# A fused attention and mixer kernel on one core: the denominator's 1e-6 moves into the PSUM evacuation, reciprocals and division move one period ahead, and weight conversion runs in four places

## The chip, the core and the metric

The kernel runs on one core of one Trainium2 chip. The metric is the device time of one execution in microseconds (us). A core has a TensorE (PE, matmuls), a VectorE (DVE), a ScalarE (ACT), a GpSimd (POOL) and a SyncE (SP), which here only issues DMAs. Each engine works through its own instruction stream in order and waits on semaphores for the others, so an instruction that waits holds back all that stand behind it on its engine.

## The reference

Shapes: attention 8 batches x 8 heads, 576 tokens, head width 64, 128 features; then two mixer blocks on (8, 576, 512).

```python
def phi(x):
    proj = np.einsum('bhsd,df->bhsf', x, w_phi)
    proj = proj - np.max(np.abs(proj), axis=-1, keepdims=True)
    return np.concatenate([np.exp(proj), np.exp(-proj)], axis=-1)
q_p, k_p = (phi(q), phi(k))
kv = np.einsum('bhsf,bhsd->bhfd', k_p, v)
z = np.sum(k_p, axis=2)
num = np.einsum('bhsf,bhfd->bhsd', q_p, kv)
den = np.einsum('bhsf,bhf->bhs', q_p, z)[..., None] + 1e-06
x = num / den
# block 1: relu(x @ w_in) split in u, v; v normalised; u * (w_spatial @ v + b_spatial); @ w_out
# block 2: u = x + (x^T @ U @ V)^T; u + relu(u @ w_ch1) @ w_ch2
```

## The kernel before

All matmul operands are float32; where one is split into a high and a low part, a product is three matmuls (high*high, high*low, low*high). The program has three stages: attention over 32 pairs of heads (two heads of 64 side by side on 128 partitions), the first mixer block with the low-rank part of the second, and the channel matmuls. The change touches the first stage only, and the helper that converts the mixer's weights from 8-byte to 4-byte floats, which runs in small steps between the attention's instructions.

`attention` (L544) is software pipelined. Loop index `p` is a period: in period `p` the core projects keys and queries of pair `p+1` (`pk`, `pq`, L396 to L400, both into one PSUM tile), subtracts the largest magnitude of each row on DVE (`m`, `s`, L405 and L408), takes exponentials on ACT (`kp` L419; `qp` high part L438; `e` L447, whose difference from the high part is the low part, made by POOL at L450), transposes queries (`pt`, L428), sums keys times values of pairs `p` and `p+1` (`pkv`, L462 and L469), and multiplies queries of pairs `p-2` and `p-1` with those sums (`pn`, L497). Each pair has four such outputs g = 0 to 3, each of six matmuls of 288 columns into the same PSUM bank `pn`; the function `outputs` returns the evacuation of that bank into the tile `nd`, which the loop calls as `taken()`: ACT copies g = 0 and 2 (L506), DVE copies g = 1 and 3 (L505). The next output cannot start until the bank has been evacuated. `split_key_values` (L482 on ACT, then L483 on DVE) empties the single bank `pkv` into the two parts of `kv`, and only then can the sums of the next pair begin at L462.

Row 64 of `nd` holds the denominators. `undivided` sends them by DMA to a tile `den9` of 128 x 9 and the numerators to `x`; `reciprocals` adds 1e-6 (L526), takes reciprocals (L527), and sends them by a DRAM tile `rd` back as the broadcast tile `rec`; `finish` multiplies on POOL (L541) and stores `x` to DRAM tile `xd`. In period `p` these belong to pairs `p-2`, `p-3` and `p-4`.

The weight jobs stand in a list: 16 pieces of `w_in`, 4 blocks of `w_spatial`, its tail and the bias, 8 pieces of `w_out`. One job occupies one period (the tail and bias two). A converted piece is done in steps, called by `step(work)` at fixed places: `words` (ACT, L55), `rounded` (DVE L60, L64, L68, and at once the ACT square L70), `kept` (DVE L77, then the split into a high part on ACT and a low part on POOL, L129 and L132). A `w_spatial` block has one step at the end of the period: DVE cast L131, POOL low part L132; its DMA (L189) needs the staging tile that the POOL low part of the block before has to give back. `load_x` (L685 to L692) brings the first batch's divided tiles back during periods 8 to 13, with a POOL subtraction at L689.

`pin` keeps the attention's own instructions in program order on each engine; a scheduler places the weight work behind the pinned instruction it was called after, and orders the DMA issues on SP.

Of the kernel before, what the change touches and what calls it, by code (L numbers as in the profile page):

```python
# [9 lines left out]
F32 = mybir.dt.float32  # L10
# [3 lines left out]
AF = mybir.ActivationFunctionType  # L14
# [4 lines left out]
P = 128  # L19
# [8 lines left out]
def fetch_weight(nc, pool, dst, src, name, at=0, raws=None):  # L28
# [7 lines left out]
    p, n = shape[0], shape[1:]  # L36
# [21 lines left out]
    def rounded(low):  # L58
        bits = tile_view(I32, 1, "bits")
        nc.vector.tensor_scalar(  # L60
            out=bits, in0=hi, scalar1=3, scalar2=0x3FFFFFF8,
            op0=ALU.logical_shift_left, op1=ALU.bitwise_and,
        )
        nc.vector.scalar_tensor_tensor(  # L64
            out=bits, in0=hi, scalar=-0x40000000, in1=bits,
            op0=ALU.bitwise_and, op1=ALU.bitwise_or,
        )
        nc.vector.tensor_tensor(out=bits, in0=bits, in1=low, op=ALU.add)  # L68
        size = low.bitcast(F32)
        nc.scalar.activation(size, hi.bitcast(F32), AF.Square)  # L70
        return lambda: kept(bits.bitcast(F32), size)
# [19 lines left out]
class Mixer:  # L91
# [259 lines left out]
    def alloc_attention(self, es):  # L351
        tc, nc = self.tc, self.nc
        D, F = self.D, self.F
        self.pp = es.enter_context(tc.tile_pool(name="pp", bufs=1, space=PSUM))
        self.af = es.enter_context(tc.tile_pool(name="af", bufs=1))
        ap = self.ap = es.enter_context(tc.tile_pool(name="ap", bufs=1))

        self.wst = ap.tile([P, F], F32, name="wst")
        nc.scalar.dma_start(self.wst, self.w_phi)
        self.st = {}  # L360

    def load(self, p, w, bufs):
# [123 lines left out]
    def outputs(self, p, g, side, n, tag="pn"):  # L486


        nc, D, HS = self.nc, self.D, self.HS
        st = self.st[p]  # L490
        qp, kv = st["qp"], st["kv"]
        if g == 0:
            st["nd"] = self.af.tile([D + 1, 4, HS], F32, tag="nd", name=f"nd{p}", bufs=2)
        pn = self.pp.tile([P, 512], F32, tag=tag, name=f"pn{p}_{g}", bufs=1)[: D + 1, :HS]
        terms = [(0, 0, 0), (1, 0, 0), (0, 0, 1), (1, 0, 1), (0, 1, 0), (0, 1, 1)]
        for m, (k, q, i) in enumerate(terms):
            self.pin(nc.tensor.matmul(  # L497
                pn, kv[k][:, i, g // 2, :], qp[q][:, i, g * HS : (g + 1) * HS],
                start=(m == 0), stop=(m == len(terms) - 1),
            ))  # L500
            if m < n:
                next(side, None)
        nd = st["nd"][:, g, :]
        if g % 2:
            return lambda: self.pin(nc.vector.tensor_copy(nd, pn))  # L505
        return lambda: self.pin(nc.scalar.copy(nd, pn))  # L506

    def undivided(self, p):

# [12 lines left out]
    def reciprocals(self, p):  # L522

        nc, D, S = self.nc, self.D, self.S
        den9 = self.st[p].pop()
        self.pin(nc.vector.tensor_scalar_add(den9, den9, 1e-6))  # L526
        self.pin(nc.vector.reciprocal(den9, den9))  # L527
        rd = self.rd[p % 4]
        nc.sync.dma_start(rd, den9)
# [14 lines left out]
    def attention(self, jobs):  # L544
# [16 lines left out]
                    return f()  # L561
            return f

        for p in range(-1, n + 5):
            tag = "pn" if p < n else "kv"
            new, this, old, older = (0 <= i < n for i in (p + 1, p, p - 1, p - 2))
            if p + 2 < n:
# [13 lines left out]
                self.load(p + 2, "v", 2)  # L581
            if new:
                self.key_features(p + 1, 0)
            if 0 <= p - 4 < n:
                self.finish(p - 4)
            work = step(work)
            taken()
            if older:
# [5 lines left out]
                self.load(p + 2, "q", 1)  # L594
            if this:
                self.high_part(p, 0)
                self.low_part(p, 0)
            less()
            side = self.key_values(p + 1, 0) if new else iter(())
            taken = self.outputs(p - 1, 0, side, 3) if old else none  # L600
# [11 lines left out]
                self.low_part(p, 1)  # L612
            work = step(work, True)
            taken()
            if 0 <= p - 3 < n:
                self.reciprocals(p - 3)
            rest = [step(f) for f in rest]
            rest = [f for f in rest if f]
            if jobs and not work:
# [474 lines left out]
```

## Time and profile before

| what | value |
|---|---|
| median of 3 runs | 1727.13 us (1726.35 to 1729.3) |
| the profiled execution's own time | 1724.92 us |
| span of its trace | 1723.1 us |
| PE busy | 1657.6 us, 96% of the span |
| DVE, ACT, POOL busy | 774.5, 594.3, 469.7 us (45%, 34%, 27%) |
| mean granted TensorE clock | 0.988 |
| chain that ended last | PE 70%, DMA 6%, DVE 4%, ACT 2%, POOL 1% |

Shares over the whole span hide that the stages differ: DVE and POOL work mostly in the first quarter. In the profile, idle time of PE is time in which no matmul was in flight; a busy PE at a granted clock below 1 is slower than it could be.

### The profile page before, as it was taken

What the parts mean: (1) busy time and instruction counts of PE and PEld (TensorE: products, weight loads), DVE (VectorE), ACT (ScalarE), POOL (GpSimd) and SP (SyncE); (2) the same over time, 40 slices, a digit from 0 to 9 for tenths busy, and PEclk for the clock granted to TensorE, in tenths of its full rate; (3) what the DMA queues carried; (4) which work ended last, traced back from release to release, by engine and by line L of the source; (5) the groups of instructions that cost most, each with busy time, mean ns of one, the idle gap of its engine ahead of it and who ended that gap; (6) DMA issues with size and microseconds to landing.
All of it is one profiled execution on the core that took longest, in us unless ns stands there. A gap on an engine that the chain in (4) does not pass through costs nothing.

```text
span 1723.1 us, 26579 instructions
## 1 busy us (share of the span) xinstructions
PE 1657.6 (96%) x10824; PEld 1568.3 (91%) x10824; DVE 774.5 (45%) x1296; ACT 594.3 (34%) x1060; POOL 469.7 (27%) x402
## 2 busy tenths in 40 slices
PE   7989988998899999999999999999999999999999
PEld 7878877887797897888898999999999999999999
DVE  5888855884667566566637211121021121121121
ACT  4767755764434443443434111021120120110110
POOL 2567665675342342342330100000000000000000
PEclk9999998999999999999999999999999999999999
DMA  4576655663223332332225201001011011011000
GB/s 131 157 186 194 194 162 152 174 176 91 77 85 108 120 103 90 119 111 70 83 68 178 64 10 37 13 26 37 1 38 37 1 37 37 1 37 37 1 19 19
DMA packets 86142, 141.41 MB, mean 82 GB/s; under 512 B 18626, under 2 KB 41314, under 8 KB 86020
## 3 DMA queue, kind: packets, MB, share of 16 engines
q1 hardware_dynamic: 85876, 139.65, 27.5%
q8 instruction: 85, 1.39, 0.3%
q14 instruction: 37, 0.30, 0.1%
q10 hardware_dynamic: 144, 0.07, 0.0%
HBM read 93.25 MB, written 36.85 MB: 75 GB/s over the span
## 4 chain that ended last, share of the span: by engine, by line
PE 70%; DMA 6%; DVE 4%; ACT 2%; POOL 1%; issue 1%; SPq 0%; DVEq 0%; POOLq 0%; ACTq 0%
PE pc L653 23%; PE ph L653 23%; PE pv L653 5%; DMA raw_c<-in_w_ch 4%; PE px L653 4%; PE pu L653 4%; PE pn L497 2%; PE pkv L469 2%; PE pt L858 1%; PE py L862 1%; PE pz L653 1%; POOL xs L689 1%; PE pv L664 1%; PE px L664 1%; PE pt L428 1%
## 5 line engine op out<-in xcount | busy, mean ns | idle before, releaser
L653 PE MATMUL pc<-h,w 128*128 128x384 f32 x2304 | 403.8, 335 | 0.0
L653 PEld LDWEIGHTS pc<-h,w 128*128 128x128 f32 x2304 | 402.0, 188 | 0.0
L653 PE MATMUL ph<-us,w 128*128 128x384 f32 x2244 | 391.0, 334 | 0.0
L653 PEld LDWEIGHTS ph<-us,w 128*128 128x128 f32 x2244 | 389.2, 188 | 0.0
L906 ACT ACTIVATE h<-ph 128x384 fp32r<-128x384 f32 x187 | 92.0, 492 | 629.5 <-PE ph L653 626.6
L497 PE MATMUL pn<-qp,kv 128*65 128x288 f32 x768 | 211.9, 335 | 24.8 <-DVE nd L505 16.7
L132 POOL TENSOR_TENSOR us<-u,us 128x384 fp32r<-128x384 f32 x48 | 48.7, 1041 | 683.0 <-ACT us L129 674.1
L907 DVE SCALAR_TENSOR_TENSOR h<-ph,h 128x384 fp32r<-128x384 f32 x187 | 104.2, 557 | 273.1 <-ACT h L906 273.0
L450 POOL TENSOR_TENSOR qp<-e,qp 128x576 fp32r<-128x576 f32 x128 | 182.3, 1453 | 46.3 <-ACT e L447 46.3
L942 DVE TENSOR_TENSOR u<-pc,u 128x384 f32<-128x384 f32 x48 | 25.7, 558 | 363.6 <-PE pc L653 363.6
L469 PEld LDWEIGHTS pkv<-v,kp 128*128 128x128 f32 x1024 | 160.2, 201 | 0.0
L469 PE MATMUL pkv<-v,kp 128*128 128x65 f32 x1024 | 160.2, 261 | 0.0
L497 PEld LDWEIGHTS pn<-qp,kv 128*65 128x65 f32 x768 | 100.8, 142 | 30.2 <-DVE nd L505 23.4
L653 PE MATMUL pz<-wt,vn 128*128 128x288 f32 x768 | 112.4, 295 | 3.2 <-DVE u L799 3.2
L653 PEld LDWEIGHTS pz<-wt,vn 128*128 128x128 f32 x768 | 105.2, 188 | 3.7 <-DVE u L799 3.6
L653 PEld LDWEIGHTS pu<-xs,wi 128*128 128x128 f32 x768 | 102.8, 188 | 3.4 <-DVE v L716 2.7
L653 PE MATMUL pu<-xs,wi 128*128 128x288 f32 x768 | 103.4, 295 | 2.5 <-DVE v L716 2.5
L653 PE MATMUL px<-wo,g 128*128 128x512 f32 x384 | 94.1, 403 | 10.5 <-ACT g L129 10.5
L653 PEld LDWEIGHTS px<-wo,g 128*128 128x128 f32 x384 | 72.9, 194 | 29.2 <-ACT g L129 13.1
L653 PE MATMUL pv<-wi,xs 128*128 128x512 f32 x384 | 92.3, 394 | 0.0
L419 ACT ACTIVATE kp<-sk 128x1152 f32<-128x1152 f32 x64 | 74.2, 1161 | 36.1 <-DVE sk L408 33.5
L653 PEld LDWEIGHTS pv<-wi,xs 128*128 128x128 f32 x384 | 71.9, 188 | 15.8
(140 smaller groups left out, 1962.0 us busy)
## 6 DMA issues: line engine op xcount, KB each, us to landing
raw_c<-in_w_ch SPq DMA_DIRECT2D x32, 512.0 KB, 4.1
v<-in_v SPq DMA_DIRECT2D x32, 325.0 KB, 3.8
k<-in_kT SPq DMA_DIRECT2D x32, 320.0 KB, 3.7
q<-in_qT SPq DMA_DIRECT2D x32, 320.0 KB, 3.4
x<-nd SPq DMA_DIRECT2D x64, 144.0 KB, 2.5
rec<-rd SPq DMA_DIRECT2D x64, 144.0 KB, 3.2
xd<-x SPq DMA_DIRECT2D x32, 288.0 KB, 2.1
x<-xd SPq DMA_DIRECT2D x32, 288.0 KB, 3.0
```

Of the source, the lines that this page charges most:

```text
L132: return (nc.gpsimd if elo == "pool" else nc.vector).tensor_tensor(out=lo, in0=src, in1=hi, op=ALU.subtract)
L419: self.pin(self.nc.scalar.activation(kp, self.st[p]["sk"], AF.Exp, scale=1.0 - 2.0 * i))
L428: self.pin(nc.tensor.transpose(pt[:, at, :], s[:, u, :], self.ident))
L450: self.pin(nc.gpsimd.tensor_tensor(out=lo[:, c], in0=e[:, c], in1=hi[:, c], op=ALU.subtract))
L469: self.pin(nc.tensor.matmul(pkv[:, i, j, :], kp[:, j * NF + t, :], vb[:, u * D1 : (u + 1) * D1], start=False, stop=(j == 1 and t == NF - 1),))
L497: self.pin(nc.tensor.matmul(pn, kv[k][:, i, g // 2, :], qp[q][:, i, g * HS : (g + 1) * HS], start=(m == 0), stop=(m == len(terms) - 1),))
L653: self.nc.tensor.matmul(out, x, y, start=(start and i == 0), stop=(stop and i == len(terms) - 1))
L664: nc.tensor.matmul(out, x, y, start=(i == 0), stop=(i == len(terms) - 1))
L689: self.nc.gpsimd.tensor_tensor(out=lo, in0=x32, in1=hi, op=ALU.subtract)
L906: nc.scalar.activation(h[:, 0, :], ph, AF.Relu)
L907: nc.vector.scalar_tensor_tensor(out=h[:, 1, :], in0=ph, scalar=0.0, in1=h[:, 0, :], op0=ALU.max, op1=ALU.subtract,)
L942: nc.vector.tensor_tensor(out=u[:, f, :], in0=pcs[f], in1=u[:, f, :], op=ALU.add)
```

## The change

The diff below is complete. The 1e-6 is added while the output leaves PSUM, from a small tile `eps` that is 1e-6 on partition 64 and zero elsewhere; of the four outputs only g = 1 leaves through DVE, the other three through ACT as an Identity activation with a bias. The separate addition on `den9` is gone. `reciprocals` handles pair `p-2` and `finish` pair `p-3`, the loop is two periods shorter, and `finish` is called after `low_part(p, 0)` in place of before the step behind `key_features`. The square becomes a step of its own (`sized`), and a fourth call of `step` stands between the high part and the low part.

```diff
@@ fetch_weight
         nc.vector.tensor_tensor(out=bits, in0=bits, in1=low, op=ALU.add)
+        return lambda: sized(bits, low)
+
+    def sized(bits, low):
         size = low.bitcast(F32)
         nc.scalar.activation(size, hi.bitcast(F32), AF.Square)
         return lambda: kept(bits.bitcast(F32), size)
@@ alloc_attention
+        self.eps = ap.tile([P, 1], F32, name="eps")
+        nc.vector.memset(self.eps, 0.0)
+        nc.vector.memset(self.eps[D : D + 1, :], 1e-6)
@@ outputs
-        if g % 2:
-            return lambda: self.pin(nc.vector.tensor_copy(nd, pn))
-        return lambda: self.pin(nc.scalar.copy(nd, pn))
+
+        if g == 1:
+            return lambda: self.pin(nc.vector.tensor_scalar_add(nd, pn, self.eps[: D + 1, :]))
+        return lambda: self.pin(
+            nc.scalar.activation(nd, pn, AF.Identity, bias=self.eps[: D + 1, :])
+        )
@@ reciprocals
-        self.pin(nc.vector.tensor_scalar_add(den9, den9, 1e-6))
         self.pin(nc.vector.reciprocal(den9, den9))
@@ attention
-        for p in range(-1, n + 5):
+        for p in range(-1, n + 3):
@@
             if new:
                 self.key_features(p + 1, 0)
-            if 0 <= p - 4 < n:
-                self.finish(p - 4)
             work = step(work)
             taken()
@@
             if this:
                 self.high_part(p, 0)
+                work = step(work)
                 self.low_part(p, 0)
+            if 0 <= p - 3 < n:
+                self.finish(p - 3)
             less()
@@
             taken()
-            if 0 <= p - 3 < n:
-                self.reciprocals(p - 3)
+            if older:
+                self.reciprocals(p - 2)
```

PE's stream keeps the same instructions in the same order. On DVE, period 14 (`kv_14` is its pair) stood so before:

```order
L408 TENSOR_TENSOR sk_2136<-pk_2112,mk_2135 128x1152
L60 TENSOR_SCALAR bits_wi_0_2168<-raw_wi_0_2108 128x256
L64 SCALAR_TENSOR_TENSOR bits_wi_0_2168<-raw_wi_0_2108,bits_wi_0_2168 128x256
L68 ISA bits_wi_0_2168<-bits_wi_0_2168,low_wi_0_2140 128x512
L505 COPY nd_2063<-pn_3_2152 65x288
L483 TENSOR_TENSOR kv_14_2180<-pkv_2066,kv_14_2179 128x260
L405 TENSOR_REDUCE mq_2202<-pq_2183 128x9
L408 TENSOR_TENSOR sq_2203<-pq_2183,mq_2202 128x1152
L77 SCALAR_TENSOR_TENSOR w_wi_0_2107<-low_wi_0_2140,bits_wi_0_2168 128x256
L505 COPY nd_2206<-pn_1_2222 65x288
L526 TENSOR_SCALAR den_11_2031<-den_11_2031 128x9
L527 RECIPROCAL den_11_2031<-den_11_2031 128x9
```

and stands so now (`pn_3` is output g = 3; the number behind `den` is the pair):

```order
L414 TENSOR_TENSOR sk_2135<-pk_2111,mk_2134 128x1152
L60 TENSOR_SCALAR bits_wi_0_2165<-raw_wi_0_2107 128x256
L64 SCALAR_TENSOR_TENSOR bits_wi_0_2165<-raw_wi_0_2107,bits_wi_0_2165 128x256
L68 ISA bits_wi_0_2165<-bits_wi_0_2165,low_wi_0_2139 128x512
L489 TENSOR_TENSOR kv_14_2176<-pkv_2066,kv_14_2175 128x260
L411 TENSOR_REDUCE mq_2201<-pq_2179 128x9
L414 TENSOR_TENSOR sq_2202<-pq_2179,mq_2201 128x1152
L80 SCALAR_TENSOR_TENSOR w_wi_0_2106<-low_wi_0_2139,bits_wi_0_2165 128x256
L512 TENSOR_SCALAR nd_2205<-pn_1_2221,eps 65x288
L535 RECIPROCAL den_12_2170<-den_12_2170 128x9
```

The evacuation of g = 3 has left DVE, so the low part of `kv` follows the rounding directly, and the reciprocal is that of the pair whose last output left PSUM in this same period.

On ACT the same period before:

```order
L419 ACTIVATE kp_15_2164<-sk_2136 128x1152
L70 ACTIVATE low_wi_0_2140<-raw_wi_0_2108 128x256
L482 CAST kv_14_2179<-pkv_2066 128x260
L438 ACTIVATE qp_14_2195<-pt_2142 128x1152
L447 ACTIVATE e_0_2198<-pt_2142 128x1152
L506 COPY nd_2206<-pn_0_2207 65x288
```

and now:

```order
L425 ACTIVATE kp_15_2163<-sk_2135 128x1152
L514 ACTIVATE nd_2063<-pn_3_2151,eps 65x288
L488 CAST kv_14_2175<-pkv_2066 128x260
L444 ACTIVATE qp_14_2191<-pt_2141 128x1152
L73 ACTIVATE low_wi_0_2139<-raw_wi_0_2107 128x256
L453 ACTIVATE e_0_2195<-pt_2141 128x1152
L514 ACTIVATE nd_2205<-pn_0_2206,eps 65x288
```

The square (L70, now L73), which needs the rounding on DVE, stood ahead of the cast of `kv` and of both exponentials; now it stands behind the cast and the high part. The evacuation of g = 3 is new here.

On POOL the same period before and the period behind it:

```order
L541 TENSOR_TENSOR x_1889<-x_1889,rec_2103 128x576
L450 TENSOR_TENSOR qp_14_2196<-e_0_2198,qp_14_2195 128x576 x2
L450 TENSOR_TENSOR qp_14_2196<-e_1_2235,qp_14_2195 128x576 x2
L132 TENSOR_TENSOR wi_116<-w_wi_0_2107,wi_115 128x256
L541 TENSOR_TENSOR x_2033<-x_2033,rec_2246 128x576
```

and now:

```order
L456 TENSOR_TENSOR qp_14_2192<-e_0_2195,qp_14_2191 128x576 x2
L549 TENSOR_TENSOR x_2030<-x_2030,rec_2102 128x576
L456 TENSOR_TENSOR qp_14_2192<-e_1_2234,qp_14_2191 128x576 x2
L135 TENSOR_TENSOR wi_116<-w_wi_0_2106,wi_115 128x256
L456 TENSOR_TENSOR qp_15_2333<-e_0_2336,qp_15_2332 128x576 x2
```

The division stood ahead of both pairs of low parts and stands between them now.

## Rows read from the trace of the kernel before

**Rows 1.** Windows: length, busy PE, PEld, DVE, ACT, POOL; PE clock, DMA share, GB/s.

```profile
38.70:70.99 32.29, 32.29 (x316) 29.57 (x315) 27.21 (x35) 25.33 (x37) 19.38 (x16) 1.00 0.50 136
70.99:193.88 122.89, 111.24 (x1051) 100.81 (x1051) 108.53 (x131) 86.69 (x125) 86.30 (x66) 0.99 0.69 190
193.88:267.35 73.47, 67.48 (x631) 62.29 (x630) 47.86 (x63) 46.14 (x59) 46.02 (x34) 0.95 0.63 175
267.35:301.24 33.89, 27.28 (x211) 25.53 (x211) 19.24 (x25) 17.41 (x24) 18.38 (x13) 0.80 0.48 139
301.24:382.67 81.43, 77.44 (x737) 70.75 (x736) 71.87 (x92) 59.19 (x85) 52.98 (x42) 0.98 0.66 176
```

**Rows 2.** Waits of PE from 70.99 to 382.67: total us, times, longest.

```profile
PE pn L497 <- DVE nd L505: 15.1, 10, 3.4
PE pkv L462 <- issue: 7.4, 15, 0.5
```

**Rows 3.** Timeline of the period from 182.13: start, duration, instruction, [idle before <-releaser].

```profile
187.33 1.58 POOL L689 TENSOR_TENSOR xs<-x,xs 128x576 fp32r<-128x576 f32 x1
187.78 1.41 DVE L68 CUSTOM_DVE_ANT_0 bits_wi<-bits_wi,low_wi 128x512 uint16<-128x512 uint16 x1
...
189.23 0.43 ACT L70 ACTIVATE low_wi<-raw_wi 128x256 f32<-128x256 f32 x1 [1.46 <-DVE bits_wi L68]
...
189.62 0.35 PE L497 MATMUL pn<-qp,kv 128*65 128x288 f32 x1 [0.23 <-DVE nd L505]
...
189.85 0.51 SPq L513 DMA_DIRECT2D den<-nd  x1
189.95 0.43 DVE L483 TENSOR_TENSOR kv<-pkv,kv 128x260 fp32r<-128x260 f32 x1 [0.39 <-ACT kv L482]
...
190.48 0.46 PE L462 MATMUL pkv<-v,kp 128*128 128x130 f32 x2 [0.52 <-issue]
...
190.84 1.13 ACT L447 ACTIVATE e<-pt 128x1152 f32<-128x1152 f32 x1
190.86 1.42 POOL L541 TENSOR_TENSOR x<-x,rec 128x576 f32<-128x576 f32 x1 [1.95 <-DMA rec<-rd]
```

**Rows 4.** Timeline of the period from 38.70, before any division, in the same columns.

```profile
44.35 0.43 DVE L68 CUSTOM_DVE_ANT_0 bits_wi<-bits_wi,low_wi 128x512 uint16<-128x512 uint16 x1
...
45.54 0.43 DVE L483 TENSOR_TENSOR kv<-pkv,kv 128x260 fp32r<-128x260 f32 x1 [0.40 <-ACT kv L482]
```

**Rows 5.** Timeline of the period from 82.76.

```profile
83.96 5.59 POOL L450 TENSOR_TENSOR qp<-e,qp 128x576 fp32r<-128x576 f32 x4
...
87.11 1.17 DVE L60 TENSOR_SCALAR bits_wi<-raw_wi 128x256 int32<-128x256 int32 x1
...
89.51 0.90 POOL L132 TENSOR_TENSOR wi<-w_wi,wi 128x256 fp32r<-128x256 f32 x1
89.97 0.73 DVE L68 CUSTOM_DVE_ANT_0 bits_wi<-bits_wi,low_wi 128x512 uint16<-128x512 uint16 x1
...
91.45 0.43 DVE L483 TENSOR_TENSOR kv<-pkv,kv 128x260 fp32r<-128x260 f32 x1 [0.39 <-ACT kv L482]
```

**Rows 6.** Timeline around the start of the period from 253.19, a block of w_spatial.

```profile
252.79 0.34 SPq L189 DMA_DIRECT2D w_wt<-in_w_spT  x1
...
255.69 0.46 DVE L131 CAST wt<-w_wt 128x576 fp32r<-128x576 f32 x1 [3.40 <-DMA w_wt<-in_w_spT]
```

**Rows 7.** DMA issues from 70 to 383: count, KB each, median us to landing.

```profile
xd<-x SPq DMA_DIRECT2D x26, 288.0 KB, 2.1
...
den<-nd SPq DMA_DIRECT2D x25, 4.5 KB, 3.3
```

**Rows 8.** Groups by line: count, busy us, mean ns of one, idle before.

```profile
L778 ACT ACTIVATE u<-pu 128x288 f32<-128x288 f32 x64 | 26.1, 410 | 58.4 <-PE pu L653 58.4
...
L506 ACT COPY nd<-pn 65x288 f32<-65x288 f32 x64 | 25.3, 395 | 70.3 <-PE pn L497 65.4 <-DMA x<-nd 4.7
...
L526 DVE TENSOR_SCALAR den<-den 128x9 f32<-128x9 f32 x32 | 19.4, 607 | 0.0
```

## The prediction

> **What bounds the kernel now.** I read the windows of the attention stage first, then PE's waits there, then three single periods. PE bounds every stage, so the change can win only what PE loses in attention: time without a matmul, and time at the lower clock. A period is counted from its first key projection (T). From 38.70 to 70.99 three periods take 32.29 us with PE never idle: 10.76 each, at full clock [rows 1]. The next ten (weight pieces of w_in) take 122.89 with 111.24 busy, so 11.65 idle; the six from 193.88 (chiefly w_spatial) take 73.47 with 5.99 idle; the two with tail and bias 33.89 with 6.61 idle; the seven from 301.24 (w_out) 81.43 with 3.99 idle [rows 1]. [...]
>
> PE's waits have two faces: the output's first matmul waits for DVE's copy of g = 3 out of the bank, and the next sums (L462) wait in 15 periods, 7.4 us in all, without a named releaser [rows 2]. The period from 182.13 names it. The rounding on DVE ends at 189.19; only then can ACT do the square at 189.23, and only behind the square the cast of kv, so that DVE's low part of kv ends at 190.38 and L462 starts at 190.48 [rows 3]. From the end of the rounding to the end of kv that is 1.19 us. PE lost 0.23 + 0.52 = 0.75 us while kv ended at T + 8.25, so PE is not held when kv ends by about T + 7.5. The undisturbed period agrees: rounding ends 44.78, kv 45.97 = T + 7.27, no idle [rows 1, 4].
>
> Why the rounding is late: the last of its three DVE operations takes 0.43 us with POOL idle and 1.41 us while POOL subtracts a tile of x for 1.58 [rows 3, 4]. From 82.76, with four low parts running one behind another until 89.55, the first takes 1.17, the rounding ends at T + 7.94 and kv at T + 9.12 [rows 5]. POOL is late there because the division in front of the low parts waits for its reciprocals to land (1.95 us of waiting before it at 190.86) [rows 3].
>
> **The change, part by part.** *kv behind the rounding.* The copy of g = 3 leaves DVE and the square no longer precedes the cast. From rounding end to kv end it is then one DVE operation, 0.43 us and a hand-over, about 0.48, against 1.19: 0.7 us less. PE is held only if the rounding ends after T + 7.0. At the old rounding ends that alone is worth the whole 7.4 us of L462's waits and some 2 of the output's [rows 2], 9.4 in all: the lower bound.
>
> *Where the rounding will end.* The first exponential ended at 191.97, T + 9.84 [rows 3]. The square's wait no longer stands before cast and high part, and kv no longer delays PE, so I put it 0.9 earlier, T + 8.9. POOL then does its pair (two at 1.40 [rows 5]), the division (1.42 [rows 3]), the second pair: 2.8 + 1.4 + 2.8 from T + 8.9 gives T + 15.9, which in a period of 10.76 is 5.2 us into the next, and the weight subtraction (0.90 [rows 5]) ends near 6.1. The rounding starts at T + 4.35 (87.11 [rows 5]); if its first two operations end with POOL's instructions, at about 5.4 and 6.4, the third ends near T + 6.9, before 7.0: no wait. In the four periods where POOL then subtracts x for 1.58 us, it ends near 7.9: 0.9 each, 3.6. I add 1.4 for periods in which POOL or a DMA runs behind. Of 11.65 + 3.99 = 15.6 idle, 10.6 go.
>
> *w_spatial.* The staging tile's DMA was issued only at 252.79, 12.1 us into its period, behind POOL's late low part; DVE's cast then waited 3.40 us for it and held the copy of g = 1, and so PE [rows 6]. With reciprocals a period ahead the division finds them landed, POOL ends the block's low part near T + 6.6, the DMA has some 3 us until the cast near T + 10: no wait. [...]
>
> [...]
>
> [...]
>
> *Costs.* The addition on den9 goes: 32 x 607 ns on DVE [rows 8], which stood before the maximum of the next keys, and that waits for PE's projection: 0 on the path (up to 0.3 a period where DVE was late). 32 evacuations move from DVE to ACT. No row has Identity with a bias tile; the nearest are the plain copy, 395 ns, and a Relu activation of as many columns, 410 [rows 8]. I take 410, bounds 395 and, doubled, 0.82. ACT was busy 86.69 of 122.89 us, 8.7 a period [rows 1]; with 0.41 + 3 x 0.015 it is 9.1 of 10.76, so nothing. The DVE addition out of PSUM reads as many columns as the copy did; at twice its time, it would still lie in the wait for the key projection. The two memsets of eps run before the first projection is there. Two loop periods less issue nothing on PE, whose order is unchanged: 0.
>
> Sum against the profiled execution, 1724.92: 10.6 + 8.9 + 4.5 = 24.0, so 1700.9. Its time lies 2.2 below the median, 1727.13; the forecast for a median is 1727.1 - 24.0 = 1703.1, **1703**.
>
> [...] At 187.78 a DVE operation took 1.41 us beside POOL in place of 0.43 [rows 3, 4]. [...]
>
> **The rivals.** *First: POOL keeps the rounding late.* The division moves 1.4 us of POOL work behind the first pair, toward the rounding. If the rounding ends where it did, 9.4 of the 15.6 idle goes, w_spatial's 8.9 go, the clock's 4.5 does not: 18.3, **1709**. For it: the 1.17 and 1.41 [rows 3, 5]. Against: the waits of the division, which made POOL late, are gone.
>
> *Second: w_spatial's wait stays,* because its DMA still follows POOL's last instruction of the period: 1703 + 8.9 = **1712**. Against: POOL should end 5 us sooner in the period.
>
> *Third, slower: the reciprocal waits on DVE.* It now takes the denominators of the same period. Before, their DMA was issued at 189.85, T + 7.7 [rows 3], and takes 3.3 us to land [rows 7], T + 11.0; the reciprocal comes about T + 11.2, and until the next projection is done, T + 12.4, its delay costs nothing. But SP must first store the divided x, whose POOL instruction is now late (near T + 2.4 of the next period), wait 2.1 us for that to land [rows 7] before it may refill the buffer, and issue keys, reciprocals and values. If all this puts the landing at T + 13.9, DVE starts the keys' maximum 1.5 us late in 25 periods, PE follows, 37.5 us: 1703 + 37.5 = **1740**. It decides at 24 / 25 = 0.96 us a period, a landing at T + 13.4; half a microsecond gives 1715.
>
> *Fourth: the waits only change their name,* ACT now holding three of four evacuations and the cast of kv behind the keys' exponential: **1727**. Against: 9.1 of 10.76.
>
> **How the numbers follow.** Forecast 0.64 (1696 to 1707), first rival 0.15, second 0.06, a mild third (around 1715) 0.06, fourth 0.03, third 0.06. The range 1695 to 1717 holds the forecast, the first two and most of the mild third, with 0.1 left out for the slow side. Two measurements of this kernel differ by up to 0.2%, 3.5 us. Faster by more than that: 0.90; within: 0.04; slower: 0.06.
>
> **What would show it.** Right: periods between 70 and 360 near 10.8 us, except two of some 17; no wait of L462 or of the output's first matmul beyond 0.9; no DVE wait for w_wt; the division without a DMA wait; the first key projection of pair 31 at about 359 in place of 382.67. Wrong: a DVE wait for den at the reciprocal, rounding ends past T + 7.0 in most periods, or periods near 11.5.

## The result, and the profile after

The changed kernel took a median of 1704.85 us over four executions (1698.59 to 1711.46) against 1727.41 for the kernel before in the same runs: a ratio of 0.987, with a 95% interval of 0.9844 to 0.9895. Run again beside the experiments it took 1703.17, a ratio of 0.9879 (0.9857 to 0.9901). 1703 had been forecast. The profiled execution took 1698.59 us, its span is 1696.8: 26.3 below the profiled execution of before, where 24.0 was summed up.

The windows of the attention stage answer to [rows 1]: three early periods, the ten with `w_in`, the six with `w_spatial`, the two with tail and bias, the seven with `w_out`.

```profile
35.29:67.80 32.51, 32.26 (x318) 29.60 (x316) 26.40 (x32) 26.80 (x40) 20.64 (x17) 1.00 0.57 154
67.80:179.00 111.20, 108.60 (x1052) 98.75 (x1051) 94.26 (x110) 91.82 (x135) 85.16 (x65) 1.00 0.74 209
179.00:245.96 66.96, 64.98 (x631) 59.24 (x630) 45.55 (x50) 49.32 (x65) 49.26 (x37) 1.00 0.69 196
245.96:279.03 33.07, 25.86 (x211) 23.89 (x211) 18.04 (x21) 18.30 (x26) 14.59 (x11) 0.85 0.51 143
279.03:355.10 76.07, 75.71 (x737) 69.04 (x736) 65.18 (x77) 62.16 (x92) 54.94 (x43) 1.00 0.68 187
```

The first window begins 0.13 ahead of its first projection; from there the three periods take 32.38, so 10.79 each.

Against [rows 1], the pieces are 11.7 us shorter (`w_in`), 6.5 (`w_spatial`), 0.8 (tail and bias) and 5.4 (`w_out`). The first projection of pair 31 stands at 355.10 in place of 382.67, so 27.6 earlier; 24.4 of that are these four. The other 3.2 lie ahead of 67.80 (70.99 before), in the start-up; behind 355.10 1341.7 us follow, 1.3 more than before.

The waits of PE between 67.8 and 355.1, and two of DVE, answer to [rows 2]: waiter, line, releaser, total, times, longest.

```profile
DVE den L535 <- DMA den<-nd: 11.8, 15, 1.9
...
PE pn L503 <- DVE nd L512: 8.5, 3, 3.9
...
DVE wt L134 <- DMA w_wt<-in_w_spT: 3.9, 4, 1.5
...
PE pkv L468 <- DVE kv L489: 2.9, 7, 0.9
```

The output's first matmul waits 3 times in place of 10, two of them in the periods of tail and bias (3.93 and 3.16), and the sums 2.9 us in place of 7.4. A new wait is that of the reciprocal for the denominators' landing: 15 times, 11.8 us.

One steady period, from T = 78.59, answers to [rows 3, 5].

```profile
79.71 1.41 POOL L549 TENSOR_TENSOR x<-x,rec 128x576 f32<-128x576 f32 x1
...
79.84 0.21 DVE L535 RECIPROCAL den<-den 128x9 f32<-128x9 f32 x1 [0.62 <-DMA den<-nd]
...
81.08 2.79 POOL L456 TENSOR_TENSOR qp<-e,qp 128x576 fp32r<-128x576 f32 x2
...
82.95 1.07 DVE L60 TENSOR_SCALAR bits_wi<-raw_wi 128x256 int32<-128x256 int32 x1
...
83.84 0.79 POOL L135 TENSOR_TENSOR wi<-w_wi,wi 128x256 fp32r<-128x256 f32 x1
...
84.06 0.84 DVE L64 SCALAR_TENSOR_TENSOR bits_wi<-raw_wi,bits_wi 128x256 int32<-128x256 int32 x1
...
84.37 0.50 ACT L514 ACTIVATE nd<-pn,eps 65x288 f32<-65x288 f32 x1
84.77 0.36 ACT L488 CAST kv<-pkv 128x260 fp32r<-128x260 f32 x1
...
85.04 0.43 DVE L68 CUSTOM_DVE_ANT_0 bits_wi<-bits_wi,low_wi 128x512 uint16<-128x512 uint16 x1
...
85.38 0.42 DVE L489 TENSOR_TENSOR kv<-pkv,kv 128x260 fp32r<-128x260 f32 x1
...
86.05 0.43 ACT L73 ACTIVATE low_wi<-raw_wi 128x256 f32<-128x256 f32 x1
```

POOL's second pair ends at 83.87, T + 5.3, the first two rounding operations end 0.15 and 0.27 behind POOL's instructions (84.02 and 84.90), the third at 85.47, T + 6.88, and `kv` at 85.80, only 0.33 later. Forecast were T + 5.2, T + 6.9 and 0.48. The cast of `kv` on ACT is long done, and the square stands behind it. The division does not wait: it starts 1.1 us into the period, right behind the first pair.

The DMA issues between 70 and 356 (count, KB each, median us to landing) answer to [rows 7], the two evacuations to [rows 8].

```profile
xd<-x SPq DMA_DIRECT2D x25, 288.0 KB, 2.5
...
den<-nd SPq DMA_DIRECT2D x25, 4.5 KB, 4.1
```

```profile
L514 ACT ACTIVATE nd<-pn,eps 65x288 f32<-65x288 f32 x75 | 37.3, 497 | 54.1 <-PE pn L503 51.7
...
L512 DVE TENSOR_SCALAR nd<-pn,eps 65x288 f32<-65x288 f32 x25 | 12.8, 511 | 6.2 <-PE pn L503 6.1
```

### The profile page after: what moved, and what is told of

It reads as the page before. It is cut to its first block, busy times and chain, and to the rows that moved or that the text cites. A ratio compares the mean times of both kernels' runs of the same rounds, so it can differ in the third digit from the quotient of the medians.

```text
span 1696.8 us, 26606 instructions
## 1 busy us (share of the span) xinstructions
PE 1649.7 (97%) x10824; PEld 1559.9 (92%) x10824; DVE 741.5 (44%) x1234; ACT 609.4 (36%) x1092; POOL 470.4 (28%) x402
## 4 chain that ended last, share of the span: by engine, by line
PE 78%; DMA 9%; DVE 4%; ACT 4%; issue 2%; POOL 2%; SPq 1%; DVEq 0%; POOLq 0%; ACTq 0%
PE pc L662 24%; PE ph L662 23%; DMA raw_c<-in_w_ch 5%; PE pu L662 4%; PE pn L503 4%; PE pv L662 4%; PE pkv L475 4%; PE px L662 4%; PE pz L662 2%; PE pk L402 1%; PE pt L434 1%; PE pt L867 1%; PE pq L402 1%; PE py L871 1%; DMA den<-nd 1%
## 5 line engine op out<-in xcount | busy, mean ns | idle before, releaser
L475 PE MATMUL pkv<-v,kp 128*128 128x65 f32 x1024 | 156.2, 256 | 0.0
L475 PEld LDWEIGHTS pkv<-v,kp 128*128 128x128 f32 x1024 | 155.4, 196 | 0.0
L503 PEld LDWEIGHTS pn<-qp,kv 128*65 128x65 f32 x768 | 101.4, 143 | 19.3 <-DVE nd L512 11.7
L662 PEld LDWEIGHTS pv<-wi,xs 128*128 128x128 f32 x384 | 72.0, 188 | 15.6
```

Of the source, the lines that this page charges most:

```text
L475: self.pin(nc.tensor.matmul(pkv[:, i, j, :], kp[:, j * NF + t, :], vb[:, u * D1 : (u + 1) * D1], start=False, stop=(j == 1 and t == NF - 1),))
L503: self.pin(nc.tensor.matmul(pn, kv[k][:, i, g // 2, :], qp[q][:, i, g * HS : (g + 1) * HS], start=(m == 0), stop=(m == len(terms) - 1),))
L662: self.nc.tensor.matmul(out, x, y, start=(start and i == 0), stop=(stop and i == len(terms) - 1))
```

## The experiments

The diff has three parts. **Evacuation**: `eps`, the new `outputs`, no addition in `reciprocals`. **Square**: `sized` as a step of its own and the fourth call of `step`. **Ahead**: reciprocals and division a period earlier, and the division's new place. Each is run alone and each is left out once; then come runs on the changed kernel. Ratios are to the kernel before, run beside, with 95% intervals. Its medians there lie between 1723.3 and 1731.2, so versions are compared by ratio. T is the first key projection of a period throughout.

| run | parts | median us | ratio |
|---|---|---|---|
| e1_evac_only | evacuation | 1729.4 | 1.0012 (0.9997 to 1.0027) |
| e2_square_only | square | 1726.81 | 0.9994 (0.9977 to 1.0012) |
| e3_ahead_only | ahead | 1718.64 | 0.9958 (0.9937 to 0.9978) |
| e6_no_ahead | evacuation, square | 1723.81 | 0.9988 (0.997 to 1.0005) |
| e5_no_square | evacuation, ahead | 1729.65 | 1.0031 (1.0017 to 1.0045) |
| e4_no_evac | square, ahead | 1710.86 | 0.9917 (0.9887 to 0.9948) |
| e0_again | all three | 1703.17 | 0.9879 (0.9857 to 0.9901) |
| e7_late_behind | all, late steps moved | 1697.31 | 0.9841 (0.9826 to 0.9856) |
| e8_division_first | all, division in front | 1730.25 | 1.004 (1.0016 to 1.0064) |
| e9_x_later | e7, x tiles later | 1696.55 | 0.9838 (0.9792 to 0.9884) |
| e10_act_order | e9, ACT's order | 1686.53 | 0.9762 (0.9722 to 0.9801) |
| e11_copies | all, plain copies | 1699.39 | 0.9829 (0.9804 to 0.9855) |

### Each part alone

Against the kernel before, the first run has only these lines (and the tile `eps` with its two memsets):

```diff
-        if g % 2:
-            return lambda: self.pin(nc.vector.tensor_copy(nd, pn))
-        return lambda: self.pin(nc.scalar.copy(nd, pn))
+        if g == 1:
+            return lambda: self.pin(nc.vector.tensor_scalar_add(nd, pn, self.eps[: D + 1, :]))
+        return lambda: self.pin(nc.scalar.activation(nd, pn, AF.Identity, bias=self.eps[: D + 1, :]))
...
-        self.pin(nc.vector.tensor_scalar_add(den9, den9, 1e-6))
```

> The kernel before with the evacuation alone: 1e-6 added on the way out of PSUM, g = 3 out through ACT, no addition on den9. The square stays glued to the rounding. Theory (what counts is the path from the end of the rounding to the end of kv): ACT now does square, evacuation of g = 3 and cast of kv one behind another, about 0.43 + 0.3 + 0.3 us, then DVE 0.43: some 1.45 us in place of 1.19, so 0.3 us later in the 15 periods that wait, +4 us: 1731 (1726 to 1735), with the clock's share open. Rival (what counts is that DVE is rid of a copy of 0.45 and an addition of 0.61 us a period): some 10 us shorter, 1717.

The second run:

```diff
+        return lambda: sized(bits, low)
+
+    def sized(bits, low):
...
                 self.high_part(p, 0)
+                work = step(work)
                 self.low_part(p, 0)
```

> The kernel before with the square alone as a step of its own behind the high part. Theory: the cast of kv no longer waits for the square, but the low part of kv still stands behind DVE's copy of g = 3, so from rounding end to kv end 0.05 + 0.45 + 0.43 = 0.9 us in place of 1.19: 0.3 us less in 15 periods, -4 us and perhaps a little of the clock: 1723 (1718 to 1726). Rival (the square's wait on ACT is the whole of it): the 15.6 us of idle in these periods go, 1712.

The third (its loop is also two periods shorter):

```diff
-            if 0 <= p - 4 < n:
-                self.finish(p - 4)
...
                 self.low_part(p, 0)
+            if 0 <= p - 3 < n:
+                self.finish(p - 3)
...
-                self.reciprocals(p - 3)
+                self.reciprocals(p - 2)
```

> The kernel before with reciprocals and division one period ahead and the division between the low parts, nothing else. Theory: rounding ends settle at T + 6.9 (7.4 to 7.9 in the four periods with x on POOL), kv ends 1.19 later, so every rounding period waits some 0.5 us and those four 1.1 to 1.6: about 12.5 us of idle against 15.6; w_spatial's waits and their clock go (7 us): 1717 (1711 to 1722). Rival (most of the gain is POOL's and DMA's, not the path behind the rounding): 1705.

Evacuation alone and square alone change nothing that can be measured. In the first, undisturbed periods take 11.24 us in place of 10.76, since 1.57 us lie between rounding and `kv`, as its theory had it; the `w_in` and `w_out` windows are 7.6 us longer, and the `w_spatial` periods 4.9 shorter. The second missed its range: undisturbed periods take 10.53, but the division in front of the low parts still waits for `rec` (65.1 us in 12 waits) and holds the others. Ahead alone gives 0.4%, inside its range, with its rounding ending at T + 6.85 and a wait of the sums of 0.53 in each `w_in` period, since 1.19 us still lie between rounding and `kv`. The three ratios together would make 0.9964; all three parts at once make 0.9879.

### Each part left out

The edits are those above, two at a time.

> The changed kernel with reciprocals and division back where they were (period p - 3 and p - 4, division ahead of the low parts). Theory: rounding ends as before (T + 6.1 to 8.4), kv 0.48 behind them: 9.4 us of 15.6 idle go, and perhaps 2 of the clock; w_spatial's waits stay: 1716 (1711 to 1720). Rival (the path behind the rounding is all): 1707.

This missed by 8 us. Its waits between 70 and 380 show why:

```profile
POOL x L549 <- DMA rec<-rd: 60.0, 15, 6.3
```

The division again stands in front of the low parts and waits for its reciprocals. In the first periods PE runs without a wait of the sums, so each period is shorter; then the division falls behind and takes the low parts and the rounding with it: rounding ends go from T + 6.08 to 8.04, 8.65 and, at worst, 9.60. The idle time of PE in the ten `w_in` periods is 10.9 us, hardly below the 11.65 of before. A shorter way from rounding to `kv` alone does not make periods shorter; it moves the hold to POOL.

> The changed kernel with the square back behind the rounding in one step. Theory: ACT does square, g = 3, cast behind the rounding: kv ends 1.45 behind T + 6.9, at T + 8.3, 0.8 us of wait in 14 periods, 1.4 to 1.9 in four: about 17 us of idle in place of 3, +14 against the changed kernel: 1719 (1713 to 1726). Rival (the step's place is a detail, the evacuation is what counts): 1706.

This was expected at 1719, below the kernel before, and came out 0.3% above it. ACT, DVE and PE in the period from 84.74, in three views:

```profile
91.55 0.43 ACT L70 ACTIVATE low_wi<-raw_wi 128x256 f32<-128x256 f32 x1 [1.17 <-DVE bits_wi L68]
91.89 0.48 ACT L511 ACTIVATE nd<-pn,eps 65x288 f32<-65x288 f32 x1
92.27 0.36 ACT L485 CAST kv<-pkv 128x260 fp32r<-128x260 f32 x1
```

```profile
91.09 0.42 DVE L68 CUSTOM_DVE_ANT_0 bits_wi<-bits_wi,low_wi 128x512 uint16<-128x512 uint16 x1
92.66 0.43 DVE L486 TENSOR_TENSOR kv<-pkv,kv 128x260 fp32r<-128x260 f32 x1 [1.15 <-ACT kv L485]
```

```profile
92.42 0.34 PE L500 MATMUL pn<-qp,kv 128*65 128x288 f32 x1 [0.42 <-ACT nd L511]
93.15 0.49 PE L465 MATMUL pkv<-v,kp 128*128 128x130 f32 x2 [0.38 <-DVE kv L486]
```

The rounding ends early, at T + 6.78, but the square waits for it, and now both the evacuation of g = 3 and the cast of `kv` stand behind the square on ACT. From rounding to `kv` it is 1.58 us, more than the 1.19 of before, and PE waits twice, 0.80 in an undisturbed period. So moving the copy from DVE to ACT helps only if the square leaves its place.

> The changed kernel with the old evacuation (g = 1 and 3 through DVE, addition on den9). Theory: rounding ends at T + 6.9, kv then 0.9 behind it at T + 7.8, 0.3 us of wait in some 14 periods and 0.8 to 1.3 in the four with x: about 7 us of idle in place of 3: +4 against the changed kernel, 1709 (1704 to 1713). Rival (the addition on den9 in front of the keys' maximum was on the path too): another 0.3 us in 25 periods, 1716.

The time is in the range, but 7.7 us above the changed kernel run beside, where 4 were expected. The theory's part is there: with the copy of g = 3 on DVE, behind the rounding, the output waits 0.2 us for it in six of the periods, where the rounding ends at T + 7.0, and up to 1.5 in those with x tiles. The rival's part is there too: in three periods the denominators land late, the addition and the keys' maximum follow, and the query projection, which needs the PSUM tile that the keys leave, holds PE for 4.4 us. Here is the addition in one of them, and PE's wait:

```profile
152.31 1.11 DVE L529 TENSOR_SCALAR den<-den 128x9 f32<-128x9 f32 x1 [2.56 <-DMA den<-nd]
```

```profile
PE pq L399 <- issue: 4.4, 3, 1.8
```

The changed kernel was run once more beside it.

> The changed kernel as it is, beside the others of this call. Its executions so far lie between 1698.6 and 1711.5 us, those of before within 3 us. Theory: the spread is the clock's: how early it rises at the start (3.2 us apart in the two traces) and when it falls behind the two periods of tail and bias; attention up to the first key projection of pair 31 then differs between executions by some us at equal waits, and the rest by as much again. Rival: DMA landings (den, w_wt) differ and with them the waits in attention. 1705 (1699 to 1711).

Its profiled execution has the same span, 1696.9, but got there in another way: its six `w_spatial` periods take 73.4 us, as before, because the wait for the staging tile's DMA [rows 6] came back in two of them, while tail and bias took 30.5 and all behind attention 1337.9. Both causes of the expectation are there: the DMA landings in `w_spatial`, and the clock in the period of the bias, granted at 1.00 for 14.15 us in place of 0.80 for 16.68; the two starts do not differ, and the granted clock is not seen to rise there: it reads 1.00 from 8 to 35 us in the traces of before, of after and of this run. Here is the cast in the first of the two:

```profile
203.39 1.33 DVE L134 CAST wt<-w_wt 128x576 fp32r<-128x576 f32 x1 [3.12 <-DMA w_wt<-in_w_spT]
```

### The late steps of tail and bias

```diff
-            work = step(work, True)
+            late_one = getattr(work, "late", False)
+            if not late_one:
+                work = step(work, True)
             taken()
+            if late_one:
+                work = step(work, True)
```

> The changed kernel, with the steps marked late (w_spatial blocks, tail, bias) called behind the evacuation of g = 1 in place of ahead of it. Theory: the waits of 3.9 and 3.3 us in the two periods of tail and bias are the evacuation of g = 1 behind DVE's late steps (1.5 and 1.2 us, themselves waiting for ACT); with them behind it, the keys' maximum is late instead, but PE has some 5 us of other work before that matters: most of 7 us of idle and of 5 us at the low clock go: 1695 (1690 to 1700). Rival: the wait only moves to the keys' maximum and then to L468, 1703.

The late steps, those of the four `w_spatial` blocks too, now stand behind the evacuation of g = 1. The two periods of tail and bias take 28.9 us in place of 33.07, and the median falls by 5.9 against the changed kernel run beside. PE's idle time there fell from 7.2 to 2.7; the clock's 5 us, which the theory had counted in, did not come: the granted clock is 0.82, PE's busy time 26.16 in place of 25.86.

### The division in front of the low parts

```diff
             if new:
                 self.key_features(p + 1, 0)
+            if 0 <= p - 3 < n:
+                self.finish(p - 3)
             work = step(work)
...
                 self.low_part(p, 0)
-            if 0 <= p - 3 < n:
-                self.finish(p - 3)
```

> The changed kernel with the division of pair p - 3 put back where the kernel before had its division: ahead of undivided() and of the first low parts, the reciprocals still one period ahead. Theory (a chain through SP closes within one period): SP issues in program order, so the store of the divided x now stands ahead of the denominators' DMA. In the changed kernel's trace the reciprocal ends about 0.2 after the denominators land, its two DMAs take 2.5 and 3.7, the division 1.4, the denominators' DMA 4.5 (3.3 before): with hand-overs 12 to 13 us for a loop that must fit one period. It no longer fits 10.79: periods of 12 to 13, a DVE wait for den ahead of the reciprocal in nearly every period, the rounding later than T + 7; some 24 periods by 1.2 or more: 1730 to 1750. Rival (only POOL's contention matters): the division lies in POOL's idle 1.8 us ahead of the first pair, the second pair ends 1.4 earlier, the rounding ends at T + 6.1 to 6.4, in the four x periods below 7.0, and their waits go: 1700 to 1702.

Slower than before, at the low end of what the theory gave. Part of the waits, then SP and POOL in one cycle:

```profile
POOL x L549 <- DMA rec<-rd: 77.6, 16, 6.4
```

```profile
114.13 0.34 SPq L550 DMA_DIRECT2D xd<-x  x1
...
116.74 0.48 SPq L525 DMA_DIRECT2D x<-nd  x1
117.31 0.54 SPq L537 DMA_DIRECT2D rd<-den  x1
...
121.13 1.11 SPq L541 DMA_DIRECT2D rec<-rd  x2
```

```profile
112.69 1.41 POOL L549 TENSOR_TENSOR x<-x,rec 128x576 f32<-128x576 f32 x1 [3.18 <-DMA v<-in_v]
...
125.46 1.42 POOL L549 TENSOR_TENSOR x<-x,rec 128x576 f32<-128x576 f32 x1 [4.98 <-DMA rec<-rd]
```

From one division to the next it is 12.77 us: the division ends at 114.10 and lets SP store `x`; that store lands at 116.60, SP refills a buffer of x at 116.74, and only behind this does it issue `rd`, at 117.31, though the reciprocal (116.12, 0.20 long) was done 1 us before; `rd` and `rec` then take 8 us together to land. A loop of 12.77 does not fit a period of 10.8, so the division falls back step by step, until a period pays for it: `w_in` periods between 10.8 and 17.1. The loop runs through SP, not through POOL's load. The wait of the reciprocal for `den`, which the theory wanted in nearly every period, came in 10 of 25 only. It is where the division stands relative to the low parts that lets the earlier reciprocals pay.

### The x tiles four periods later

```diff
-            if 0 <= p - late < self.KD:
-                rest.append(self.load_x(0, p - late))
+            if 0 <= p - late - 4 < self.KD:
+                rest.append(self.load_x(0, p - late - 4))
```

> The kernel with the late steps behind the evacuation of g = 1, and besides the four tiles of x loaded and split four periods later, where no rounding runs. Theory (POOL's 1.58 us subtraction of x holds the rounding's operations): the four x periods now end their rounding at T + 6.9 in place of 7.4 to 7.9, without a wait of the sums (2.4 us there in the late-steps run), all w_in periods 10.8: about 1695. Rival (the x loads and POOL's subtraction only collide elsewhere, with the low parts of w_spatial's blocks): the w_in periods are clean, but waits of 2 us or more come up in the w_spatial periods: 1698 to 1702.

Both held in part. In the four periods where POOL had subtracted tiles of x, the rounding now ends at T + 6.84 to 6.89 (one at 7.15), and of the four the sums wait in that one alone, 0.38; PE's idle time over the ten `w_in` periods falls from 2.5 in e7 to 1.1. But the first of the moved tiles fell into the last period with a rounding of `w_in`, which now ends it at T + 7.86, where the sums wait 0.87, and the six periods from there take 0.6 more. The median does not tell it from the kernel with the late steps moved.

### ACT's order, and plain copies

The first has the x tiles later, the late steps moved, and besides:

```diff
+            if this:
+                self.split_key_values(p)
             taken()
             if older:
                 self.undivided(p - 2)
-            if this:
-                self.split_key_values(p)
...
                 self.high_part(p, 0)
-                work = step(work)
                 self.low_part(p, 0)
...
             taken()
+            if this:
+                work = step(work)
             taken = self.outputs(p - 1, 1, side, 6, tag) if old else none
```

> The kernel with the x tiles four periods later, and besides two instructions moved on ACT alone: the cast of kv ahead of the evacuation of g = 3, and the square behind the evacuation of g = 0. Theory (ACT's chain sets the clean period: with a third evacuation, at 0.50 us each, kv's cast starts at T + 6.18 in place of 5.79 and g = 0's evacuation at 8.79 in place of 8.65, and PE's L503 behind it starts at 9.35 in place of 9.10, all from the traces of the changed kernel and of the one without the moved evacuations): the clean periods fall from 10.79 to 10.54 or 10.6, some 24 of them by 0.2 to 0.25: 5 to 6 us below the 1696.5 of the kernel with the x tiles later, 1690 to 1692. Rival (ACT has room, as the prediction had it; the 10.79 comes from the rounding's end at T + 6.87): periods stay at 10.79, 1696.

The best version of the study: 1686.53, a ratio of 0.9762 (0.9722 to 0.9801). Its windows over the same stretches of work (`w_in`, `w_spatial`, tail and bias, `w_out`), then those of e9, on which it builds:

```profile
69.40:176.90 107.50, 107.32 (x1051) 98.68 (x1050) 87.21 (x110) 90.21 (x132) 78.26 (x61) 1.00 0.73 205
176.90:244.90 68.00, 65.23 (x631) 59.35 (x630) 47.08 (x50) 50.35 (x68) 55.25 (x41) 1.00 0.75 215
244.90:270.40 25.50, 21.98 (x213) 19.87 (x212) 17.41 (x21) 17.94 (x26) 14.90 (x11) 1.00 0.63 166
270.40:346.50 76.10, 74.98 (x736) 69.01 (x735) 61.61 (x77) 62.62 (x92) 55.03 (x43) 1.00 0.68 190
```

```profile
67.70:177.20 109.50, 108.41 (x1051) 98.76 (x1050) 92.66 (x110) 89.65 (x132) 78.31 (x61) 1.00 0.72 203
177.20:245.00 67.80, 65.31 (x631) 59.35 (x630) 45.33 (x50) 50.65 (x68) 55.40 (x41) 1.00 0.73 210
245.00:273.20 28.20, 25.05 (x213) 22.50 (x212) 17.28 (x21) 19.93 (x28) 17.28 (x12) 0.89 0.61 170
273.20:348.90 75.70, 75.58 (x736) 69.25 (x735) 63.65 (x77) 60.72 (x91) 52.38 (x42) 1.00 0.67 188
```

Clean periods fell from 10.79 to 10.64, 0.15 where 0.2 to 0.25 was expected, and only eight of the 17 `w_in` and `w_out` periods are clean, not 24. The ten `w_in` periods are 2.0 shorter; besides the clean ones, late denominators cost less there (with the reciprocal at T + 2.3 in both, a period takes 10.94 in place of 11.29). Tail and bias are 2.7 shorter, but that is the clock: PE's idle time there did not fall, and its busy time went from 25.05 to 21.98 with the granted clock at 1.00 in place of 0.89. `w_out` is 0.4 longer (one period of 12.00), `w_spatial` 0.2, the start 1.7. The stage behind attention, which the edit does not touch, took 10.1 less in this profiled execution. So the order on ACT is shown to be worth some 2 us, in the `w_in` periods; the rest of the 10 between the two medians is not shown to be its doing, and the two intervals just overlap.

The second goes back to copies on the changed kernel:

```diff
         if g == 1:
-            return lambda: self.pin(nc.vector.tensor_scalar_add(nd, pn, self.eps[: D + 1, :]))
-        return lambda: self.pin(
-            nc.scalar.activation(nd, pn, AF.Identity, bias=self.eps[: D + 1, :])
-        )
+            return lambda: self.pin(nc.vector.tensor_copy(nd, pn))
+        return lambda: self.pin(nc.scalar.copy(nd, pn))
...
+        self.pin(nc.vector.tensor_scalar_add(den9, den9, 1e-6))
         self.pin(nc.vector.reciprocal(den9, den9))
```

> The changed kernel with its evacuations on the same engines but without eps (plain copies), and the 1e-6 added to den9 on DVE ahead of the reciprocal, as in the kernel before. Theory (what the evacuation part gives is the 128x9 addition that leaves the denominators' way: it starts when they land, at T + 1.2, beside POOL's division, and lasts until that ends, so the keys' maximum comes up to 1.1 late): periods without division 10.6, with division 11.0 to 11.3, a few tenths of PE's waits in each: 1709 to 1713, as the run without the evacuation part (1711). Rival (the addition costs nothing, as the prediction had it, and the part's worth is that the copy of g = 3 leaves DVE): the copies are 0.1 us shorter each on ACT than the additions, periods 10.6 to 10.8: 1699 to 1703.

The rival's number came. The theory's mechanism is there too, in the period from 89.35:

```profile
91.09 0.93 DVE L533 TENSOR_SCALAR den<-den 128x9 f32<-128x9 f32 x1 [1.18 <-DMA den<-nd]
92.06 0.22 DVE L534 RECIPROCAL den<-den 128x9 f32<-128x9 f32 x1
92.19 1.30 DVE L411 TENSOR_REDUCE mk<-pk 128x9 f32<-128x1152 f32 x1
```

The addition lasts until POOL's division ends at 91.99, the keys' maximum starts 1.2 later in its period than in the changed kernel, and the period takes 11.50. But that happens in four periods (a fifth takes 11.29), and three undisturbed ones fall from 10.79 to 10.6, as the copies are 0.10 shorter; five stay at 10.8. Together the `w_in` and `w_out` windows take 189.3 us, where the changed kernel has 187.3 and, in e0_again, 187.4, so folding the 1e-6 into the evacuation gains 2 us there. The profiled executions have the same span all the same (1696.4 and 1696.8), and by the ratio the plain copies are no slower: their interval overlaps that of the first result and lies just below that of e0_again. What the evacuation part brings to the time is the move of g = 3 from DVE to ACT, the one thing in which e4 and e11 differ: 0.9917 (0.9887 to 0.9948) against 0.9829 (0.9804 to 0.9855).

## Why the prediction was right, and where it was not

**The terms.** PE's idle time in the `w_in` and `w_out` windows is 111.20 - 108.60 + 76.07 - 75.71 = 2.96 us; 12.7 of the 15.6 went, where 10.6 was summed. The sum's 4.5 for the clock is the author's estimate, and no run shows it by itself. What the windows of before take beyond idle time and 10.76 a period is 122.89 - 11.65 - 107.6 = 3.6 in `w_in` and 81.43 - 3.99 - 75.3 = 2.1 in `w_out` [rows 1]; 1.0 and 0.4 of it are left, at a granted clock of 1.00 in both windows: 4.3 won, where 4.5 was. Before, each of these windows has one stretch at a granted clock of 0.50, 165.7 to 169.2 behind gaps of PE of 1.11 and 0.52 us and 356.9 to 360.3 behind gaps of 1.00 and 0.52; at half the clock the two cost 3.4 of the 4.3. The sum's 8.9 is 5.99 of idle time and 73.47 - 5.99 - 64.6 = 2.9 beyond it, at a mean clock of 0.95 [rows 1]. `w_spatial` gave 6.5 of this 8.9 in this execution, and nothing in the profiled one of e0_again. POOL's low part ends at T + 6.5 in both, as forecast; the step that was off is the DMA behind it, which was to have "some 3 us until the cast" and took 3.3 to 5.6 us to land, in e0_again 4.3 to 5.7. Tail and bias, for which the sum has no term since the late steps still stand ahead of g = 1 there, gave 0.8. Unforecast were 3.2 from the start-up and 1.3 lost behind attention. 12.7 + 4.3 + 6.5 + 0.8 + 3.2 - 1.3 = 26.2, which is the 26.3 of the two executions but for rounding. That the sum came so near is in part luck: the start-up, which the change does not explain, gave 3.2, about what `w_spatial` fell short and the stage behind attention lost.

**Rounding and POOL.** The chain from the first exponential was right to a tenth: T + 8.9, T + 5.3, T + 6.88. What DVE loses beside POOL [rows 3, 5] did not decide, though it is there: the first operation of the rounding takes 1.07 beside POOL's pair and ends 0.15 behind it. The third runs alone, at 0.43, since POOL's weight subtraction is over by then. In the four x periods the rounding ended at T + 7.38 to 7.86, as said, and their waits came to 2.0, not 3.6. Taken out by e9, they are gone.

**Which step failed: the lower bound.** The prediction had it that "At the old rounding ends that alone is worth the whole 7.4 us of L462's waits and some 2 of the output's [rows 2], 9.4 in all: the lower bound." e6_no_ahead has the short way from rounding to `kv` and is worth 0.12% (interval -0.05 to 0.3), not 9.4 us: the rounding's end does not stay where it was. It hangs on POOL, POOL on the division, the division on reciprocals of a loop through two DMAs. The forecast did not rest on that bound, but the first rival's 1709 did.

**ACT at nothing.** The evacuation with a bias takes 497 ns, not 410, and "9.1 of 10.76, so nothing" was wrong: an engine with over 1.5 us to spare in a period can still be the last in a chain. `kv`'s cast starts behind the third evacuation, and e10 gets 0.15 a period back by changing only ACT's order. The clean periods show it as well: 10.76 before, 10.53 in e2 and e4 (the square moved, the copy of g = 3 still on DVE), 10.60 in e11 (that copy on ACT), 10.79 with all parts: the evacuation part, the bias above all, gives back what the square's move had won there. A plain copy took 395 [rows 8], 393 in e11, and the Identity with a bias tile 497: 102 to 104 ns more, which no row of before could give.

**The rivals.** POOL keeping the rounding late (1709) did not come. `w_spatial`'s wait (1712) came in the profiled execution of e0_again and not in the other, where the six periods took 6.4 us less, so its chance was too low as a yes or no; it is one cause for executions that differ by up to 13 us. The reciprocal did come to wait for `den`, as the slower rival said, but the landing at about T + 12 stays ahead of the keys' projection, and only two of the 17 periods with a rounding pay for it (11.55 and 11.30). The same rival's path, SP's order with the division ahead of it, is real: e8 has it and is slower than before. The addition on `den9` was not free either: where denominators land late it holds the query projection, as e4 shows. The fourth (1727) came only where parts are missing: with the square in its old place, e5, ACT's order holds PE in all 17 periods with `w_in` and `w_out`.

**What was to show it.** Of the 25 periods between 67.80 and 355.10, 15 take 10.65 to 10.95 us, and the two with tail and bias 16.4 and 16.7, as said. Eight are longer: the four x periods (11.30 to 11.77), which the sum had counted, and two with late denominators and two of `w_spatial` (12.23 and 11.47), which it had not. Outside tail and bias the output's first matmul waited once beyond 0.9, 1.38 in `w_spatial`. The division waits for no DMA; two waits of POOL ahead of low parts the profile puts down to `rec`, 4.8 us in all. One sign of being wrong came and meant little: DVE waits for `den` at the reciprocal, but that wait lies for the most part in the wait for the keys' projection. DVE's wait for `w_wt` did not vanish, 3.9 us in four. Pair 31 came at 355.10, not 359, of which the start-up explains 3.2.

## What to carry to other kernels

When several engines form a loop around a software-pipelined period (here reciprocal, DMA, DMA, division, low parts, rounding, sums), edits to single links can be worth nothing or cost time, as e1, e2, e5 and e6 show (ratios 1.0012, 0.9994, 1.0031 and 0.9988), since the next link holds; price such edits together, by adding up the loop and comparing it with the period. A DMA queue's program order is part of that loop: where a store waits for a slow engine, what is issued behind it waits too, as `rd` did in e8, for 1 us. And spare time in an engine's period says little (ACT had over 1.5 us, and its order alone won 0.15 a period in e10); read what stands ahead of the one instruction that others wait for.

## What was not expected of the hardware

A DVE instruction of nine columns is held like a large one, but not every one. All additions on `den` and all reciprocals in the trace of before (count; shortest, median and longest in ns; first and last start):

```profile
L526 DVE TENSOR_SCALAR den<-den x32: 154/686/1245, 60.7 to 422.6; 128x9 f32<-128x9 f32 x32
L527 DVE RECIPROCAL den<-den x32: 215/216/218, 61.4 to 423.5; 128x9 f32<-128x9 f32 x32
```

Eight of the additions take 154 to 160 ns. The other 24 start while a POOL instruction runs and end 0.03 to 0.04 us behind it, whatever is left of it; so does the addition in e11 that took 0.93 (92.02, POOL's division 91.99). The reciprocal of the same nine columns takes 215 to 218 ns each time, though POOL is at work all through 20 of the 32. This adds to [rows 3, 4], where a rounding took 1.41 in place of 0.43. What holds the additions and that rounding and does not hold the reciprocal, no row shows.

The start-up is 3.2 us shorter in the changed kernel, and not for any work that left it. The matmuls of the first sums took 274 ns each between 8 and 22 us, 407 before, at a granted clock of 1.00 in the records of both:

```profile
L475 PE MATMUL pkv<-v,kp 128*128 128x65 f32 x32 | 3.9, 274 | 0.0
```

```profile
L469 PE MATMUL pkv<-v,kp 128*128 128x65 f32 x20 | 4.5, 407 | 0.0
```

Runs with either start are among the experiments: the second period takes 9.2 to 9.6 us in eight of them and 10.4 to 11.8 in e3, e4, e5 and e10. What decides it stays open.

DMAs took longer to land at shorter periods: denominators 4.1 us for 3.3, the stores of x 2.5 for 2.1 [rows 7], while the `w_in` windows went from 190 to 209 GB/s.
